# Which engines wait for which output store ahead of the last branch, in a fused attention and maxout kernel on one core

## The chip, the cores and the metric

The kernel runs on one core of a Trainium2 chip. The metric is the device time of one execution in microseconds, and the number compared is the median of several executions.

## The reference

Eight batches of eight heads, sequence length 1024, head size 64; E and F shorten the keys and values from 1024 to 64 rows; a maxout layer follows on the 8192 tokens. The output is 8192 x 512 in float32 (16.8 MB).

```python
k_proj = np.einsum('ks,bhsd->bhkd', E, k)
v_proj = np.einsum('ks,bhsd->bhkd', F, v)
scores = scale * np.matmul(q, k_proj.transpose(0, 1, 3, 2))
attn = softmax(scores)                       # with 1e-9 added to the sum
attn_out = np.matmul(attn, v_proj)           # regrouped to x: 8192 tokens x 512
h1 = x @ w1; h2 = x @ w2                     # 512 -> 1024
out = np.maximum(h1, h2) @ w_out             # 1024 -> 512
```

## The kernel before

**The bulk.** The tokens are worked through in 16 units of 512. For each unit TensorE makes scores, softmax sums, attention outputs, the up products and the down products; the products are built in a scheme with seven block products per pair of matrices (`product`, L747 for the up side, L839 for the down side). ScalarE empties PSUM banks (`keep`, L721) and computes the exponentials, VectorE adds block products (L870, L914, L938) and makes the operand sums. An explicit list of slots (`slots`, `steps`) fixes the order of all instructions on all engines; the change doesn't touch it.

**The last unit.** It is treated apart (`alone`): its output leaves in smaller pieces, so that little is left after the last matmul. `store` (L855) issues one DMA from SBUF to DRAM per piece, on the queue of SyncE (SP) or of ScalarE, and keeps the names of the latest four stores in `ends_of`:

```python
ends_of[:] = [*ends_of[-3:], ins.ins.name]
```

The last five stores are, in order: two of product 3 (128 KB each, on SP and then on ScalarE's queue), and three of product 4 (128 KB on SP, 64 KB on ScalarE's queue, 64 KB on SP). When the program text is complete, `ends_of[0]` is therefore the second store of product 3, on ScalarE's queue; `ends_of[1]` is the 128 KB store of product 4, on SP's queue.

**The guard.** The fast way leaves out the subtraction of the maximum in the softmax. `step_guard` and `step_flag` test the sums of all exponentials and put into `flag` how many rows fell out of a range. At the end every engine loads the flag into a register (L1196 for VectorE, ScalarE and GpSimd, L1180 for SyncE and TensorE, where it stands earlier) and branches on it (L1210): when the flag is zero it jumps over a second, slow version of the whole computation (`tile_shifted`), which has code on all five engines. After the jump each engine has a few semaphore instructions, the program's end barrier (L1363), which SyncE enters only after it has checked the semaphore of every DMA queue and of every engine, and then code that isn't the kernel's.

**The waits ahead of the branch.** Between the register loads and the branch stand three instructions that compute nothing that is used. Each waits for `ends_of[1]`, the third last store, so that its engine comes to the branch only once that store has landed: a one-column matmul on TensorE (L1199), a memset of one element on VectorE (L1200), a copy of one element on ScalarE (L1201). SyncE and GpSimd have no such instruction.

Of the kernel before, what the change touches and what calls it, by code (L numbers as in the profile page):

```python
# [9 lines left out]
FP32 = mybir.dt.float32  # L10
FP16 = mybir.dt.float16
I32 = mybir.dt.int32
# [7 lines left out]
def kernel(  # L20
# [12 lines left out]
    nc = tc.nc  # L33
# [12 lines left out]
    scale = 1.0 / float(D) ** 0.5  # L46

    guard = ctx.enter_context(tc.tile_pool(name="guard", bufs=1))
    flag_ended = guard.tile([1, 4], I32, name="flag")
    flag = flag_ended[:, 0:1]  # L50
    ended = flag_ended.bitcast(FP32)
    outer, ctx = ctx, ExitStack()
    const = ctx.enter_context(tc.tile_pool(name="const", bufs=1))
    kvq = ctx.enter_context(tc.tile_pool(name="kvq", bufs=4))
# [12 lines left out]
    def mm_bank(dtype=FP32, n=None):  # L67
        if n is None:
            n = turn.pop(0)
            turn.append(n)  # L70
        return ps.tile([128, 512 if dtype == FP32 else 1024], dtype, tag=f"mm{n}", name="mm_ps")
# [9 lines left out]
    def big(n, dtype=FP16):  # L81
# [11 lines left out]
            name=nc.get_next_instruction_name(),  # L93
            act_func_set_id=LN_EXP_SET,
            engine=mybir.EngineType.Activation,
            ins=[],
# [33 lines left out]
    for g in range(2):  # L130
        for w_sb, w in ((w2_sb, moe_w2), (w1_sb, moe_w1)):
            nc.gpsimd.dma_start(
                out=w_sb.rearrange("p (g z) f -> p g z f", z=2)[:, g, :, 0:256],
                in_=w.rearrange("(g p z) f -> p g z f", p=128, z=2)[:, g, :, 0:256],
            )
    for w_sb, w, f0, f1 in (
# [3 lines left out]
        for z in range(2):  # L140
            nc.gpsimd.dma_start(
                out=w_sb.rearrange("p (g z) f -> p g z f", z=2)[:, :, z, f0:f1],
                in_=w.rearrange("(g p z) f -> p g z f", p=128, z=2)[:, :, z, f0:f1],
# [3 lines left out]
    ones16 = const.tile([128, 512], FP16)  # L147
# [1034 lines left out]
    ends_of = []  # L1182
# [12 lines left out]
        if reg.engine not in (mybir.EngineType.SP, mybir.EngineType.PE):  # L1195
            nc.reg_load(reg, flag)  # L1196

    for ins in (
        nc.tensor.matmul(out=mm_bank()[0:1, 0:1], lhsT=ones16[:, 0:1], rhs=ones16[:, 0:1], start=True, stop=True),  # L1199
        nc.vector.memset(ended[:, 1:2], 0.0),  # L1200
        nc.scalar.copy(out=ended[:, 2:3], in_=flag),  # L1201
    ):
        for x in ends_of[1:2]:
            tc.add_manual_dep(
                ins.ins, x, mybir.DependencyInfo(mybir.DependencyClass.Sync, mybir.DependencyReason.DATA),
                reason="fetches of instructions wait for the stores",
            )
    ctx.close()

    with tc.If(nc.snap(regs, min_val=0, max_val=256), preferred_fallthrough_block=True, label="shifted"):  # L1210
# [157 lines left out]
```

## Time and profile before

| what | value |
|---|---|
| median of 3 runs | 320.11 us (320.11, 320.11, 320.31) |
| the profiled execution | 320.41 us |
| its span, first to last instruction of the program | 318.6 us |
| around the span | 1.8 us |
| granted TensorE clock | 1.00 |
| TensorE matmul busy | 312.2 us (98%) |
| VectorE, ScalarE busy | 241.3 us (76%), 206.4 us (65%) |
| last matmul of the computation starts, ends | 314.85, 315.13 us |
| the three waiting instructions start | 316.87 to 316.90 us |

The page of the profile gives the busy time of each engine and the chain of work that ended last. Times inside an execution are counted from the start of the span. An engine name with a small q (SPq, DVEq) is that engine's sequencer: branches, semaphore instructions, register loads and the issue of DMAs, none of which counts as busy time.

### The profile page before, as it was taken

The page shows a single profiled execution, that of the slowest core. Times are in us where ns is not written, and L with a number is a line of the kernel's source. Part 1 is how long each engine was busy: PE and PEld are TensorE (multiplying, and loading weights), DVE is VectorE, ACT ScalarE, POOL GpSimd, SP SyncE. Part 2 cuts the span into 40 slices and gives each one's busy share as a digit, 9 for nine tenths or more (in the row PEclk, how much of TensorE's full clock was granted, in tenths as well). Part 3 has the DMA queues.
Part 4 walks back from the last instruction along what each step waited for, and adds up shares of the span by engine and source line. Part 5 has one row for each costly group of instructions (what it writes and reads, how often), then busy time and mean ns, then how long its engine had stood idle before and what let it go on. Part 6 is the DMA issues. An engine that isn't in the chain of part 4 may idle for free.

```text
span 318.6 us, 9311 instructions
## 1 busy us (share of the span) xinstructions
PE 312.2 (98%) x3922; PEld 253.7 (80%) x3922; DVE 241.3 (76%) x442; ACT 206.4 (65%) x374; POOL 40.2 (13%) x63
## 2 busy tenths in 40 slices
PE   8989999999999999999999999999999999999995
PEld 3555588788887888788887888788887888888885
DVE  2365888877969696996969696996969696969873
ACT  2466842777776777477776777477776777765541
POOL 8259002003000300030000400030000000000000
PEclk9999999999999999999999999999999999999999
DMA  7999999999959999899999899989969131313133
GB/s 191 208 198 196 206 206 202 207 167 171 207 109 196 166 208 245 211 178 164 231 222 214 167 205 246 214 145 184 232 145 210 44 102 35 102 35 102 36 115 119
DMA packets 76684, 53.71 MB, mean 169 GB/s; under 512 B 29664, under 2 KB 76128, under 8 KB 76640
## 3 DMA queue, kind: packets, MB, share of 16 engines
q0 software_dynamic: 30688, 28.05, 55.7%
q1 hardware_dynamic: 45664, 24.85, 32.1%
q8 instruction: 31, 0.51, 0.6%
q10 hardware_dynamic: 288, 0.20, 0.2%
q14 instruction: 13, 0.11, 0.1%
HBM read 57.15 MB, written 16.78 MB: 232 GB/s over the span
## 4 chain that ended last, share of the span: by engine, by line
PE 90%; DMA 7%; POOL 1%; DVE 1%; issue 0%; ACT 0%; DVEq 0%; POOLq 0%
PE mm_ps L839 47%; PE mm_ps L747 27%; PE mm_ps L526 4%; DMA q_sb<-in_q_dram 3%; PE att_ps L354 3%; DMA big<-in_moe_w_dram 3%; PE mm_ps L197 3%; PE mm_ps L342 2%; PE mm_ps L635 2%; PE att_ps L239 1%; PE mm_ps L313 1%; DMA out_dram<-o_sb 1%; POOL k_sb L110 0%; DVE xt_sb L445 0%; PE mm_ps L558 0%
## 5 line engine op out<-in xcount | busy, mean ns | idle before, releaser
L721 ACT COPY p_sb<-mm_ps 128x512 f32<-128x512 f32 x179 | 101.8, 592 | 49.0 <-PE mm_ps L747 27.2
L839 PEld LDWEIGHTS <-big 128*128 128x128 f16 x768 | 73.5, 98 | 11.8 <-issue 3.6
L839 PE MATMUL mm_ps<-T_sb,big 128*128 128x256 f16 x576 | 76.9, 273 | 0.0
L762 DVE TENSOR_TENSOR gt_sb<-mm_ps,p_sb 128x512 f16<-128x512 f32 x56 | 38.5, 687 | 43.0 <-PE mm_ps L747 41.6
L747 PE MATMUL mm_ps<-big,big 128*128 128x256 f16 x336 | 50.4, 273 | 0.0
L747 PEld LDWEIGHTS <-big 128*128 128x128 f16 x448 | 43.8, 98 | 5.1
L839 PE MATMUL mm_ps<-wo_sb,gt_sb 128*128 128x256 f16 x256 | 42.6, 273 | 0.0
L839 PEld LDWEIGHTS <-gt_sb 128*128 128x128 f16 x376 | 35.7, 98 | 6.7 <-issue 2.7
L471 ACT ACTIVATE ex_sb<-mm_ps 128x512 f16<-128x512 f32 x50 | 27.2, 596 | 18.0 <-PE mm_ps L342 12.3
L747 PEld LDWEIGHTS <-wd_sb 128*128 128x128 f16 x336 | 32.9, 98 | 3.8
L747 PE MATMUL mm_ps<-xt_sb,wd_sb 128*128 128x256 f16 x224 | 32.8, 273 | 0.0
L501 DVE TENSOR_TENSOR xt_sb<-att_ps,ld_sb 128x1024 f16<-128x1024 f32 x26 | 31.6, 1217 | 0.2
L839 PE MATMUL mm_ps<-m_sb,xt_sb 128*128 128x256 f16 x128 | 24.4, 273 | 0.0
L305 POOL COPY junk<-qt_sb 1x1 f16<-1x1 f16 x6 | 2.0, 340 | 174.1 <-DMA qt_sb<-q_sb 174.1
L870 DVE TENSOR_TENSOR o_sb<-mm_ps,p_sb 128x512 f32<-128x512 f32 x32 | 21.8, 682 | 2.8 <-ACT p_sb L899 2.0
L765 DVE TENSOR_SCALAR gt_sb<-gt_sb 128x512 f16<-128x512 f16 (+1 forms) x60 | 21.1, 351 | 2.1
L707 DVE TENSOR_TENSOR big<-gt_sb 128x1024 f16<-128x1024 f16 x32 | 21.8, 682 | 0.0
L839 PE MATMUL mm_ps<-wo_sb,big 128*128 128x256 f16 x128 | 21.5, 273 | 0.0
L808 ACT ACTIVATE gt_sb<-mm_ps 128x512 f16<-128x512 f32 x28 | 16.8, 601 | 5.7 <-PE mm_ps L747 5.7
L839 PE MATMUL mm_ps<-T_sb,gt_sb 128*128 128x256 f16 x120 | 20.3, 273 | 0.0
L839 PEld LDWEIGHTS <-xt_sb 128*128 128x128 f16 x188 | 18.3, 98 | 2.3 <-issue 0.2
L762 DVE TENSOR_TENSOR gt_sb<-p_sb 128x512 f16<-128x512 f32 x28 | 19.1, 681 | 0.6 <-ACT p_sb L721 0.6
(123 smaller groups left out, 434.2 us busy)
## 6 DMA issues: line engine op xcount, KB each, us to landing
out_dram<-o_sb SPq DMA_DIRECT2D x62, 256.0 KB
k_sb<-in_k_dram POOLq DMA_DIRECT2D x7, 1024.0 KB, 10.0
v_sb<-in_v_dram POOLq DMA_DIRECT2D x7, 1024.0 KB, 16.0
q_sb<-in_q_dram POOLq DMA_DIRECT2D x5, 1024.0 KB, 23.6
q_sb<-in_q_dram POOLq DMA_DIRECT2D x6, 512.0 KB, 15.6
big<-in_moe_w_dram POOLq DMA_DIRECT2D x12, 128.0 KB, 6.4
v_sb<-in_v_dram POOLq DMA_DIRECT2D x4, 256.0 KB, 13.4
wo_sb<-in_moe_w_out_dram POOLq DMA_DIRECT2D x1, 1024.0 KB, 10.1
```

The costliest lines, as they stand in the source:

```text
L197: nc.tensor.matmul(out=kv_ps[r * KP : (r + 1) * KP, h * D : (h + nh) * D], lhsT=eft[i][:, c, :], rhs=t[w][:, h0 + h : h0 + h + nh, c, :], ...
L471: nc.scalar.activation(out=t["ex", g, j][:, e, :], in_=banks[e], func=ACTF.Exp, scale=scale)
L501: nc.vector.tensor_tensor(out=x_out(t, g, j).rearrange("q z o n -> q o z n"), in0=at_ps.rearrange("q o (z n) -> q o z n", z=2), in1=ld[:, ...
L526: nc.tensor.matmul(out=h_ps, lhsT=wd_sb[:, r, fb * 128 : (fb + 1) * 128], rhs=t["xt"][:, r, :, j * W : (j + 1) * W], start=(r == 0), stop= ...
L707: nc.vector.tensor_tensor(out=S(i), in0=S(0) if x is None else x, in1=y(), op=op)
L721: copy(out=x, in_=bank)
L747: nc.tensor.matmul(out=bank[:, m * W : (m + 1) * W], lhsT=w_[:, n_, (2 * d + m) * 128 : (2 * d + m + 1) * 128], rhs=a[:, n_, :], start=(n ...
L762: nc.vector.tensor_tensor(out=c_blk(j, c), in0=two(x), in1=two(y), op=ALU.add)
L765: nc.vector.tensor_scalar_max(ap, ap, 0.0)
L808: nc.scalar.activation(out=out, in_=in_, func=ACTF.Relu)
L839: nc.tensor.matmul(out=bank[i][:, 0:CH] if two_banks else bank[:, i * CH : (i + 1) * CH], lhsT=a(c)[:, i * 128 : (i + 1) * 128], rhs=w_(c) ...
L870: nc.vector.tensor_tensor(out=o_sb, in0=two(x), in1=two(y), op=ALU.add)
```

## The change

VectorE's memset and ScalarE's copy are taken out, with the two views of the flag tile that they wrote to. TensorE's one-column matmul stays where it is, and waits for `ends_of[0]`, the fourth last store (128 KB, on ScalarE's queue), in place of `ends_of[1]` (128 KB, on SP's queue). VectorE and ScalarE go from the load of the flag to the branch with no wait for a store.

```diff
-    flag_ended = guard.tile([1, 4], I32, name="flag")
-    flag = flag_ended[:, 0:1]
-    ended = flag_ended.bitcast(FP32)
+    flag = guard.tile([1, 1], I32, name="flag")
...
-    for ins in (
-        nc.tensor.matmul(out=mm_bank()[0:1, 0:1], lhsT=ones16[:, 0:1], rhs=ones16[:, 0:1], start=True, stop=True),
-        nc.vector.memset(ended[:, 1:2], 0.0),
-        nc.scalar.copy(out=ended[:, 2:3], in_=flag),
-    ):
-        for x in ends_of[1:2]:
-            tc.add_manual_dep(
-                ins.ins, x, mybir.DependencyInfo(mybir.DependencyClass.Sync, mybir.DependencyReason.DATA),
-                reason="fetches of instructions wait for the stores",
-            )
+    ins = nc.tensor.matmul(
+        out=mm_bank()[0:1, 0:1], lhsT=ones16[:, 0:1], rhs=ones16[:, 0:1], start=True, stop=True
+    )
+    tc.add_manual_dep(
+        ins.ins, ends_of[0],
+        mybir.DependencyInfo(mybir.DependencyClass.Sync, mybir.DependencyReason.DATA),
+        reason="a fetch of instructions waits for a store",
+    )
     ctx.close()
```

## The prediction

> **What bounds the kernel now.** I read the page first, to see whether the edit touches what fills the time.
>
> ```profile
> span 318.6 us, 9311 instructions
> ...
> PE 312.2 (98%) x3922; PEld 253.7 (80%) x3922; DVE 241.3 (76%) x442; ACT 206.4 (65%) x374; POOL 40.2 (13%) x63
> ...
> PE 90%; DMA 7%; POOL 1%; DVE 1%; issue 0%; ACT 0%; DVEq 0%; POOLq 0%
> ```
>
> TensorE bounds the kernel, and the edit takes no matmul from it: up to the last matmul of the computation (ends 315.13) nothing differs. What can move is the last 3.5 us of the span (315.13 to 318.63) and the 1.78 us around it (320.41 - 318.63). So the second view is the chain of waits for the end:
>
> ```profile
> 314.55 0.65 DVE o_sb L938 x3
> 315.20 1.72 DMA out_dram<-o_sb
> 316.93 0.17 ACT flag L1201
> ```
>
> The end hangs on stores in flight. The list of waits from 314 us on says which instructions they hold, and what SyncE's own queue waits for:
>
> ```profile
> ACT flag L1201 <- DMA out_dram<-o_sb: 3.0, 1, 3.0
> PEld L1199 <- DMA out_dram<-o_sb: 1.9, 1, 1.9
> ...
> DVE flag L1200 <- DMA out_dram<-o_sb: 1.4, 1, 1.4
> ...
> SPq L1363 <- DVEq L1210: 0.5, 1, 0.5
> ```
>
> The last line is the one that matters: SyncE, checking everything before the end barrier, stands 0.5 us for VectorE's first instruction after the branch, not for a DMA. The busy times by stretch show whether data still moves by then:
>
> ```profile
> 315.90:316.30 0.40, 0.00 (x0) 0.00 (x0) 0.00 (x0) 0.00 (x0) 0.00 (x0) 1.00 0.99 320
> 316.30:316.90 0.60, 0.03 (x1) 0.03 (x1) 0.03 (x1) 0.00 (x0) 0.00 (x0) 1.00 0.78 212
> 316.90:317.20 0.30, 0.14 (x1) 0.05 (x1) 0.03 (x1) 0.19 (x1) 0.00 (x0) 1.00 0.00 0
> 317.20:317.90 0.70, 0.00 (x0) 0.00 (x0) 0.00 (x0) 0.00 (x0) 0.00 (x0) 1.00 0.00 0
> ```
>
> The last two columns are DMA share and GB/s: the last store's packets are through by 316.9. The semaphore updates in the trace give when each store had landed: the fourth last at 316.28, the third last at 316.83, the last two at 317.01 and 317.20. The sequencers' rows at the branch:
>
> ```profile
> L1210 DVEq COMPARE_BRANCH x1: 72/72/72, 316.9 to 316.9; - x1
> L1210 PEldq COMPARE_BRANCH x1: 383/383/383, 317.0 to 317.0; - x1
> ...
> L1210 ACTq EVENT_SEMAPHORE  x1: 17/17/17, 317.5 to 317.5; - x1
> L1210 DVEq EVENT_SEMAPHORE  x1: 21/21/21, 317.5 to 317.5; - x1
> ```
>
> VectorE branches at 316.94 (until 317.01) and runs its next instruction only at 317.54; ScalarE 316.99 and 317.46; TensorE 316.97 (383 ns) and 317.41. Last, the DMA view from 316.9 us to the end, for code fetches:
>
> ```profile
> DMA  0000000000000000000000000906000004000000
> ...
> q8 instruction: 1, 0.02, 4.0%
> q14 instruction: 2, 0.02, 2.8%
> ```
>
> A slice is 43 ns, and a packet counts where it starts: 16 KB of code starts at 318.00, 1.03 us after TensorE's branch begins; two of 8 KB start at 318.05 and 318.33. Queue 8 is TensorE's: its 31 packets bring 0.51 MB in the whole run, 65 bytes for each of TensorE's 7844 instructions; the other engines' code comes in the 8 KB packets. Here a 16 KB packet takes 4.0% x 16 x 1.7 us = 1.09 us, an 8 KB one 2.8% x 16 x 1.7 / 2 = 0.38 us.
>
> **The change, part by part.**
>
> *VectorE's memset out.* 59 ns by itself; what counts is its wait. The flag load runs 315.18 to 315.75, so the branch moves from 316.94 to about 315.9, and with the same 0.53 us behind it VectorE is through at about 316.5. SyncE asks for this at 317.08: the 0.51 us stand (317.08 to 317.59) goes. What is late next is the last store: SyncE's checks follow each other by 62 ns, it would ask for that store at 317.14, and it lands at 317.20. Then come the same steps as now: SyncE's last drain at 317.42 instead of 317.82, so the span is **0.40 us** shorter. The barrier behind it (318.63 - 317.82 = 0.81 us) stays.
>
> *ScalarE's wait and copy out.* 17 and 190 ns. The flag load ends at 316.27, the branch comes near 316.4, the first instruction after it 0.42 to 0.5 us later, at 316.9. SyncE asks for it last, at 317.29. Nothing, while 0.4 us of cover stands; left in place, the wait would give a release at 317.49, so it would have to go with VectorE's.
>
> *TensorE waits for the fourth last store.* Landed at 316.28 instead of 316.83: 0.55 us earlier. With 40 ns to react as now, branch at 316.42 to 316.80, next instruction at 316.86. SyncE's check on TensorE stands beside the last store's, so the span gains nothing more. Nothing of the computation is queued behind the matmul on TensorE. But the code fetch moves with the branch, from 318.00 to 317.45, through at 318.54 instead of 319.09.
>
> *Behind the span.* No instruction of the kernel is there, only semaphore updates: a signal passes from engine to engine twice. Its hops in the second round are 34, 38, 45 ns; in the first 34, **207**, 44. The 207 ns hop ends at 319.10, 9 ns after TensorE's fetch. If the fetch holds it, it comes at 318.55, so 0.55 us earlier, and the shorter span allows 318.86 - 0.40 + 0.07 = 318.53. If something else does, it moves with the span, by 0.40 us. The fetch fits to 9 ns, but one hop is little evidence: I take **0.50 us**, nearer to the fetch's row.
>
> [...]
>
> *The flag tile, 4 bytes instead of 16.* No row prices it; one element is read at a time. Nothing.
>
> Sum: 320.41 - 0.50 = 319.91 in the profiled execution. That one lies 0.30 us above the median, so 320.11 - 0.50 = **319.6 us**, 0.16% less. The bounds: 0.40 and 0.57 us (the hop at 318.53), so 319.5 to 319.75 for this case alone. A measurement of this kernel tells about 0.2%, 0.64 us, from no change: the forecast is a gain that hardly shows.
>
> **The rivals.**
>
> *The gain passes the bound: 319.4.* After the first round each engine clears a block of semaphores; the block that starts last does so at 319.61, 0.22 us after the round's end, where the others need at most 0.07. If this too waits for code (an 8 KB fetch starts late, at 318.84, and ends at 319.28), up to 0.15 us more can go: 0.57 + 0.15 = 0.72. For it: the fetches overlap each other here, and TensorE's takes 1.09 us where the mean of the 31 is 0.6% x 16 x 318.6 / 31 = 0.99; apart they should be shorter. Against it: nothing ties that block to a fetch.
>
> *Hidden anyway: 320.1.* SyncE needs the last store at 317.20; were that 0.39 us later, it would stand until 317.59 as now. VectorE's fetch, 1.0 to 1.4 us after a branch at 315.9, starts at 316.9 to 317.3, just when the last packets (316.85) are through. Some 0.1 us earlier, its 0.38 us fall on one DMA engine's share of that store, and eat the span's gain. Here belongs also that the edit doesn't do what it says: were ScalarE's queue drained late, TensorE would leave no sooner than now. Against both: its store landed 0.55 us before the other.
>
> *Slower: 320.8.* TensorE's own fetch falls before the last store. The 16 KB packet takes 1.09 us; put ahead of the last packets on one DMA engine it moves the landing from 317.20 to 318.29, and SyncE's release from 317.59 to 318.29, 0.70 us later than now. It decides from a fetch start before 316.85, that is within 0.43 us of the branch at 316.42. For it: the DMA engines are at a share of 0.78 to 0.99 until then, and the new wait lets TensorE go at 316.3, when 0.6 us of store packets are still to move. Against it: the fetch came 1.03 us after the branch. [...]
>
> **How the numbers follow.** Forecast 0.42; hidden anyway 0.13; both are within 0.2%, together 0.55. Gain past the bound 0.28: its terms are few and I know one execution. Slower 0.17. The range runs from the larger gain, with 0.1 us for the spread of the medians, to no gain with the 0.3 us that the profiled execution lay above: 319.3 to 320.4. It leaves out the slower case.
>
> **What would show it.** Right: in the changed profile SyncE's wait for VectorE's branch is gone from its list and the longest is for the last store; TensorE's matmul at L1199 starts at 316.3; the 16 KB fetch starts at about 317.45 in an empty DMA row; the span is 318.2. Wrong: a code fetch among the last store's packets; a landing later than 317.3; or a time around the span that differs from 1.7 us by over 0.15 us.

## The result and the profile after

The medians are 319.96 us after (319.64 to 320.28, 22 runs) and 320.40 us before (320.11 to 321.23, 22 runs). The ratio is 0.9983 with a 95% interval of 0.9977 to 0.9990: 0.54 us faster, 0.32 to 0.74 us (the two medians by themselves differ by 0.44 us). A ratio of 1 lies outside the interval; the gain itself lies under the 0.2% (0.64 us) below which the prediction took a gain to be hard to see. The profiled execution took 319.90 us, with a span of

```profile
span 318.1 us, 9308 instructions
```

The list of what SyncE's queue waits for, from 314 us on (columns: us in total, times, longest us), is where the change shows:

```profile
SPq L853 <- DVE o_sb L936: 0.9, 1, 0.9
SPq L1359 <- SPq L1359: 0.4, 1, 0.4
SPq L1359 <- PEq L1359: 0.3, 1, 0.3
SPq L1206 <- SPq L1206: 0.2, 1, 0.2
```

The line of the kernel before in which SyncE stood 0.5 us for VectorE's first instruction after the branch is gone. The lines left are the issue of the last stores (L853), the end barrier (L1359) and SyncE's own steps behind its branch (L1206), as before. A wait for the last store has no line here, because it is short: by the trace, SyncE's check for it stands 134 ns behind the one before, where 62 ns is the usual step, and 17 ns behind the landing. The sequencers' rows at the branch (L1206, count, durations in ns, first and last start):

```profile
L1206 DVEq COMPARE_BRANCH x1: 72/72/72, 315.8 to 315.8; - x1
...
L1206 ACTq COMPARE_BRANCH x1: 54/54/54, 316.3 to 316.3; - x1
L1206 PEldq COMPARE_BRANCH x1: 388/388/388, 316.3 to 316.3; - x1
L1206 DVEq EVENT_SEMAPHORE  x1: 21/21/21, 316.4 to 316.4; - x1
L1206 PEldq EVENT_SEMAPHORE  x1: 51/51/51, 316.8 to 316.8; - x1
L1206 ACTq EVENT_SEMAPHORE  x1: 17/17/17, 316.8 to 316.8; - x1
```

All three engines have run their first instruction behind the branch by 316.83; the last store landed at 317.10. The busy times by stretch (DMA share and GB/s last) and the DMA view from 316.9 to 318.6 us (slices of 43 ns) show what became of the code fetches:

```profile
316.30:316.90 0.60, 0.10 (x1) 0.01 (x1) 0.00 (x0) 0.00 (x0) 0.00 (x0) 1.00 0.63 163
316.90:317.20 0.30, 0.00 (x0) 0.00 (x0) 0.00 (x0) 0.00 (x0) 0.00 (x0) 1.00 0.14 27
```

```profile
DMA  0090000000060000000000090000000007000000
...
q14 instruction: 3, 0.02, 6.2%
q8 instruction: 1, 0.02, 3.3%
```

Three fetches of 8 KB start at 317.03, 317.41 and 318.34, and TensorE's 16 KB at 317.88. The first follows the last store packet (316.75) by 0.28 us.

Where the time went is told by one interval: from the landing of the last store to the end of the span. It was 318.63 - 317.20 = **1.43 us** before and is 318.12 - 317.10 = **1.02 us** after, 0.41 us less. The other 0.10 us between the two spans is that the last store landed earlier in the second execution; over the nine profiled executions in which that store took 1.71 or 1.72 us, it landed anywhere from 316.96 to 317.36. The time around the span is 1.78 us in both.

### The profile page after: what moved, and what is told of

Its sections match the earlier page's. It is cut to its first block, busy times and chain, and to the rows that moved or that the text cites. A ratio compares the mean times of both kernels' runs of the same rounds, so it can differ in the third digit from the quotient of the medians.

```text
span 318.1 us, 9308 instructions
## 1 busy us (share of the span) xinstructions
PE 312.3 (98%) x3922; PEld 253.6 (80%) x3922; DVE 241.1 (76%) x441; ACT 206.2 (65%) x373; POOL 40.8 (13%) x63
## 4 chain that ended last, share of the span: by engine, by line
PE 92%; DMA 5%; POOL 1%; ACT 1%; issue 0%; DVE 0%; POOLq 0%
PE mm_ps L837 47%; PE mm_ps L745 27%; PE mm_ps L524 4%; DMA v_sb<-in_v_dram 4%; PE att_ps L352 3%; PE mm_ps L195 3%; PE mm_ps L340 2%; PE mm_ps L633 2%; PE att_ps L237 1%; DMA out_dram<-o_sb 1%; PE mm_ps L311 1%; POOL k_sb L108 0%; POOL q_sb L108 0%; ACT ld_sb L388 0%; ACT ex_sb L380 0%
```

## The experiments

Theory A: the end of the span is set by SyncE's list of checks, so by whatever on it is satisfied last: VectorE's, TensorE's or ScalarE's first instruction behind the branch, or the last store. Rival B: TensorE's earlier branch and code fetch carry the gain. Rival C: code fetches among the stores hold them up, so that too early a branch costs. For each kernel the table gives, from its profiled execution, the time from the last store's issue to its landing, from the landing to the end of the span, and the ratio to the kernel before, from all its runs. The edits are shown shortened, and the first one in words.

| kernel | issue to landing | landing to end | ratio [95%] |
|---|---|---|---|
| before | 1.72 us | 1.43 us | 1 |
| changed | 1.71 | 1.02 | 0.9983 [0.9977, 0.9990] |
| changed, again | 1.72 | 1.02 | 0.9993 [0.9975, 1.0011] |
| only TensorE moved | 1.72 | 1.42 | 1.0012 [1.0003, 1.0021] |
| VectorE's and ScalarE's out | 1.72 | 1.28 | 1.0001 [0.9992, 1.0010] |
| VectorE's out | 1.71 | 1.26 | 1.0001 [0.9992, 1.0010] |
| changed, ScalarE waits | 1.72 | 1.22 | 0.9985 [0.9960, 1.0009] |
| all wait for the last store | 1.72 | 1.80 | 1.0007 [0.9981, 1.0032] |
| changed, TensorE for the fifth last | 1.72 | 1.02 | 0.9978 [0.9954, 1.0002] |
| changed, VectorE loads early | 2.57 | 1.02 | 1.0011 [0.9986, 1.0035] |
| changed, no wait at all | 3.63 | 1.02 | 1.0059 [1.0045, 1.0072] |
| before, TensorE free | 3.71 | 1.02 | 1.0049 [1.0032, 1.0066] |

Wide intervals come from single outlying runs (up to 323.84 us); what the ratios leave unclear is read from the second and third columns, which come from one execution of each kernel and leave out all that happens before the last store's issue.

**Only TensorE's wait moved.**

```diff
-        nc.tensor.matmul(...)  waits for ends_of[1]
+        nc.tensor.matmul(...)  waits for ends_of[0]
         nc.vector.memset(...)  waits for ends_of[1]
         nc.scalar.copy(...)    waits for ends_of[1]
```

> Only TensorE's matmul moves to the fourth last store; VectorE and ScalarE still wait for the third last. From the last store's landing to the end of the span it was 1.43 us in the kernel before and 1.02 in the changed one. Theory A, SyncE's list of checks: the check on VectorE still ends last, so 1.43 us again and no gain (within 0.1 us of the kernel before). Rival B, TensorE's earlier branch carries the gain: 0.2 to 0.45 us faster, with the 16 KB fetch and the end of the execution earlier.

SyncE's list still has its 0.5 us:

```profile
SPq L1362 <- DVEq L1209: 0.5, 1, 0.5
```

The interval is 1.42 us; TensorE branched at 316.52 and its fetch started at 317.55, and nothing came of it. B falls. The median is 0.24 us above that of the kernel before, by an interval that leaves out zero; the one profiled execution (320.50 us) shows no place for that, and it stays open.

**VectorE's and ScalarE's instructions out, TensorE's as before.**

```diff
-        nc.vector.memset(ended[:, 1:2], 0.0),
-        nc.scalar.copy(out=ended[:, 2:3], in_=flag),
```

> VectorE's memset and ScalarE's copy are out, TensorE still waits for the third last store. Theory A: SyncE passes VectorE at once and then stands for TensorE, whose first instruction after the branch raised its semaphore 0.09 us before VectorE's did in the kernel before; the span is about 0.12 us shorter (1.31 us behind the last landing), a third of the change's gain. Rival B: no gain at all, since TensorE branches as before. Rival D, VectorE's and ScalarE's waits alone are worth it all: the full 0.4 us.

```profile
SPq L1360 <- PEq L1207: 0.4, 1, 0.4
```

As A has it, SyncE now stands for TensorE, 0.4 us in place of 0.5; the interval is 1.28 us, a gain of 0.15 us that the ratio can't show. Two of the three waits alone are worth a third of the gain.

**VectorE's instruction out.** As above, with ScalarE's copy left in.

> Only VectorE's memset is out; TensorE and ScalarE wait for the third last store as in the kernel before. Theory A: the same 0.12 us as with ScalarE's copy out too (1.31 us behind the last landing), since TensorE's check comes ahead of ScalarE's and holds both. Rival D: the full 0.4 us.

1.26 us, and the same line for TensorE in SyncE's list. Again A; VectorE's wait is not worth it all.

**The changed kernel with ScalarE's wait.** TensorE on the fourth last store, VectorE free, ScalarE's copy kept on the third last.

> As the changed kernel, but ScalarE's copy stays and waits for the third last store. Theory A, SyncE's list: ScalarE's first instruction after the branch comes at about 317.47 as in the kernel before, SyncE asks for it last and gets it there; about 1.23 us from the last landing to the end of the span, between the kernel before (1.43) and the changed one (1.02), so half of the gain. Rival: ScalarE's wait is covered and costs nothing, 1.02 us.

```profile
SPq L1361 <- ACTq L1208: 0.2, 1, 0.2
```

1.22 us: half of the gain, with ScalarE now the last on the list. So TensorE's wait holds the end when VectorE is free, and ScalarE's when the other two are out of the way; that VectorE's does follows from the first run, where its check ends last and costs 0.2 us more than ScalarE's alone. Only with all three out of the way is it the store.

**All three wait for the last store.**

```diff
-        for x in ends_of[1:2]:
+        for x in ends_of[3:4]:
```

> As the kernel before, but all three instructions wait for the last store (landed 317.20) in place of the third last (316.83). Theory A: VectorE's branch and SyncE's release move by the same 0.37 us, 1.80 us from the last landing to the end of the span, 0.37 us slower than the kernel before. Rival E, later branches are cheaper than they look because fetches meet no store: less than 0.15 us slower.

```profile
SPq L1362 <- DVEq L1209: 0.9, 1, 0.9
```

1.80 us, to the hundredth what A said; the medians differ by 0.5 us (320.94 and 320.43), though the interval of the ratio includes 1. E falls by SyncE's list, not by the times.

**No wait at all.** The matmul stays, without its dependency.

```diff
-    tc.add_manual_dep(ins.ins, ends_of[0], ...)
```

> As the changed kernel, but TensorE's matmul waits for no store either, so TensorE branches at about 315.3 us, before the last four stores have moved. Theory A: nothing more to gain, 1.02 us behind the last landing, the changed kernel's time. Rival C, the code fetch falls among the stores: a 16 KB packet of 0.9 to 1.1 us stands ahead of store packets on one DMA engine, the last store lands 0.4 to 1.1 us later after its issue (1.72 us in the kernel before) and the time is 0.4 to 1.1 us longer than the changed kernel's.

```profile
SPq L1354 <- DMA out_dram<-o_sb: 2.0, 1, 2.0
```

The median is 322.13 us, 1.7 us above the kernel before. TensorE branched at 315.34. The other packets of the last stores were through at 316.86, but nine of them, 4 KB, a sixteenth of the last store's 144 packets, moved only from 317.97 to 318.45, and the store landed at 319.13, 3.63 us after its issue. SyncE stands 2.0 us for it. C holds as far as it goes, but the landing is 1.91 us late where 0.4 to 1.1 us were expected, and all three engines fetch code here, so this run doesn't tell whose fetch it is.

**The kernel before with TensorE alone set free.** VectorE and ScalarE keep their waits.

> As the kernel before, but TensorE's matmul waits for no store; VectorE and ScalarE still wait for the third last, so that TensorE's 16 KB fetch is the only one among the stores. With no wait and all three fetches early the last store landed 3.63 us after its issue in place of 1.72, its late packets moving from 317.97 on, when all three fetches were through. Theory F1, TensorE's fetch alone does it: the landing is 0.9 to 1.3 us late (one packet of 0.9 to 1.1 us and the order behind it), 1.02 us from it to the end. Theory F2, the 8 KB fetches of the other two hold the store as much: with them kept back the landing is late by less than 0.6 us, and the time is within 0.3 us of the kernel before.

The GB/s row of its DMA view from 315.3 to 319.3 us (slices of 0.1 us):

```profile
GB/s 328 164 82 307 369 328 292 272 282 256 261 139 5 0 0 164 0 0 0 0 0 0 0 5 5 174 10 5 5 0 0 0 0 0 0 0 0 0 0 0
...
q8 instruction: 1, 0.02, 1.4%
```

The store packets end at 316.54; then comes the 16 KB fetch (316.83 to 317.71, slice 16), and only then, at 5 to 10 GB/s, the nine packets left over. The two 8 KB fetches (slice 26) come at 317.81, too late to have held these packets back. So TensorE's early branch and its fetch do it alone, as F1 says, but the landing is 1.98 us late and not 0.9 to 1.3: the nine packets don't move while the fetch is under way nor in the 0.29 us before its packet, and they land 0.66 us after the last of them where 0.35 us is usual. The parts add up: 0.29 us ahead of the fetch's packet, 0.86 until the first of the nine starts (317.70), 0.53 for the nine, 0.31 of later landing. Why nothing moves in the first of these parts, and why the landing takes longer, the trace doesn't show. The fetch's one packet took 0.88 us, less than half of the delay measured.

**TensorE waits for the fifth last store.**

```diff
-                ends_of[:] = [*ends_of[-3:], ins.ins.name]
+                ends_of[:] = [*ends_of[-4:], ins.ins.name]
```

> As the changed kernel, but TensorE waits for the fifth last store (landed at 315.9 us), so it branches at about 316.0, 0.35 us sooner. By theory A nothing is gained (1.02 us behind the last landing, the changed kernel's time), as long as the code fetch stays out of the last store. With 1.03 us from a free branch to its fetch (kernel before, and TensorE's wait moved alone), the fetch would start at 317.05, after the last packets at 316.8, and the time is the changed kernel's. Rival C2, what counts is when the fetch is asked for, not when its packet starts: asked for while store packets are still queued, it goes ahead of one DMA engine's share of the last store, which then lands about 2 us later as without any wait, and the time is 1.5 to 2.2 us longer.

```profile
GB/s 338 277 92 184 317 348 318 297 292 277 272 251 67 0 0 164 82 0 0 82 0 0 0 0 0 0 0 0 0 0 82 0 0 0 0 0 0 0 0 0
```

The same slices as above: the stores are through at 316.61, the fetch starts at 316.88 (slice 16), 1.04 us after the branch at 315.85, and nothing is left over. 1.02 us, the changed kernel's. C2 falls for this branch: 0.77 us ahead of the end of the store packets it is still harmless. The two branches that did harm came 1.52 us (no wait) and 1.47 us (TensorE free) ahead of the end of the other store packets.

**VectorE loads the flag earlier.**

```diff
-        at = {SP: ("U", last - 1, 1, 4), PE: ("P", last, 5, 0)}.get(reg.engine)
+        at = {SP: ("U", last - 1, 1, 4), PE: ("P", last, 5, 0), DVE: ("P", last, 5, 0)}.get(reg.engine)
```

> As the changed kernel, but VectorE loads the flag earlier, in the third last product, as TensorE does, so that VectorE branches at about 315.2 to 315.3 us in place of 315.8; its 8 KB fetch then is asked for 0.5 us sooner, among the last stores. Theory A without collision: the changed kernel's time, 1.02 us behind the last landing. Rival C, an 8 KB fetch (0.4 to 0.7 us) goes ahead of one DMA engine's share of the last store: the last landing 0.4 to 1.5 us later, and the time as much longer.

```profile
SPq L853 <- DVE o_sb L936: 1.3, 1, 1.3
SPq L1360 <- DMA out_dram<-o_sb: 0.9, 2, 0.8
```

VectorE branched at 314.98 and its 8 KB fetch started at 316.50, among the store packets. The last store landed 2.57 us after its issue, 0.85 us late. The load itself made VectorE's last additions, and with them the issue of the last three stores, later: the first two by 0.32 us, the last by 0.28 (SyncE waits 1.3 us for an addition in the first line, 0.9 in the other kernels). With the 0.41 us of the changed kernel that makes 0.28 + 0.85 - 0.41 = 0.72 us; the medians differ by 0.78 us. So an 8 KB fetch among the stores goes with a late landing too: nine packets of the store before the last, a sixteenth of it, move only from 316.87 on, when the fetch ends, and nine of the last store behind them, from 317.18 to 317.50. But TensorE's 16 KB fetch starts at 317.17 and runs beside those last packets, which then land 0.56 us behind the last of them and not 0.35. How the 0.85 us divide between the two fetches isn't shown.

**The changed kernel again.**

> The changed kernel once more, on the chip and beside the runs of this call. By SyncE's list 1.02 us from the last landing to the end of the span, 0.4 us less than the kernel before, ratio 0.9987; if half of the measured gain was the chip's or the day's, 0.2 us or less.

The medians are 320.00 and 320.31 us; the ratio is unclear (one run of 322.72 us). The medians by themselves, 0.31 us apart, lie between the two expectations. The interval of 1.02 us is that of the first execution to 1 ns, so the 0.41 us at the end of the span belong to the code.

## Why the prediction was right, step by step

*The step from VectorE's check to the last store* was to take 0.40 us from the span. Measured: 0.41. Branch and next instruction came at 315.81 and 316.41 (315.9 and 316.5 were worked out), SyncE's last drain 0.22 us after the last landing, as the 62 ns steps gave. Of the signs that the prediction named, VectorE's line is gone from SyncE's list, TensorE's matmul started at 316.23 (316.3) and the span is 318.1 us (318.2). The wait for the last store is too short to stand in the list, and the time around the span stayed at 1.78 us and didn't come down to 1.7.

*The share of the three edits* was told wrongly. The prediction gave the whole to VectorE and wrote that TensorE's wait adds nothing to the span. It is worth nothing alone (1.42), but VectorE's alone is worth 0.16 us, because TensorE would be next on the list at 317.5. The prediction named this cover for ScalarE, with its release at 317.49, and the run with ScalarE's wait bears it out (1.22); for TensorE it forgot it. The smaller flag tile isn't where the rest lies: the kernel before with TensorE alone set free has the old tile, and 1.02 us once the store is last.

*The code fetch* was to move with the branch to 317.45. It came at 317.88, 1.55 us after the branch, in a row with three other fetches and not in an empty one. An 8 KB fetch (317.41, 0.47 us) ended at that moment, but that isn't shown to be the cause: in the second execution of the same kernel TensorE's fetch started at 317.62, 1.05 us after its branch, with an 8 KB fetch still under way (317.24 to 317.74). The prediction's 1.03 us holds to 0.02 us in eight of the twelve executions; the others are 1.53 (all three wait for the last store), 1.55 here, and 1.64 and 1.77 us in the two collisions.

*The late hop behind the span* was the one term that failed: 0.10 us were booked for it. The hop is 208 ns in the changed kernel too, ending at 318.59, before the fetch is through (318.79); it is 207 or 208 ns in every kernel here, whatever the fetch does. So it is no wait for that fetch; the 9 ns were a coincidence. The sum should have been 0.40 us; the forecast of 0.50 lies inside the measured 0.32 to 0.74, and so does 0.41, so that the times alone couldn't have told the two apart.

*The forecast of 319.6 us* stands on the median of three runs, 320.11 us. The 22 runs beside the changed kernel give 320.40 us for the kernel before, so the profiled execution of 320.41 us didn't lie 0.30 us high: the base was 0.29 us low. With 320.40 us for the base and 0.40 us for the gain the sum is 320.00 us, next to the measured 319.96. That value lies outside the narrow bounds of 319.5 to 319.75 us and inside the stated range only because of its upper part, which was meant for a gain that stays hidden: for the time itself that is luck, for the gain it isn't.

*The first instructions behind the branch* didn't wait for a code fetch in the executions named here. In the kernel before, TensorE ran on at 317.41 and its fetch started at 318.00; without any wait it ran on at 315.79, 1.2 us before its fetch started. The kernel marks this branch as likely taken for TensorE; what the mark does isn't shown, since every run has it. VectorE has no such mark, and in the changed kernel it ran on at 316.41, while no code fetch stands in the trace between 303.0 and 317.03. What the 0.53 us behind its branch are, the same in eleven of the twelve executions, stays open.

*The rivals.* More than the bound: nothing came out of the time around the span, 1.77 to 1.86 us in all. Hidden anyway: the first 8 KB fetch, taken as VectorE's, missed the last packets by 0.28 us. Slower: too early a branch of TensorE does make the last store land late, but that was priced at less than half: 0.70 us worked out, 1.6 and 1.7 us measured. The 0.70 us stand on an estimate, that the fetch delays the landing by the 1.09 us of its own packet; no run shows a delay of that size: with TensorE free the packet took 0.88 us and the landing came 1.98 us late. The sign given for it, a fetch that starts before the last packets, isn't what the runs show: in the two runs in which TensorE branched too early, its fetch's packet itself started late, 0.12 and 0.29 us behind the other store packets. What tells the cases apart is the branch. With 1.03 us from branch to fetch the bound would be a branch 1.03 us ahead of the end of the store packets, and the runs put it between 0.77 us (harmless) and 1.47 us (held). The changed kernel's TensorE branches 0.41 us ahead.

## What to carry to other kernels

When an end barrier checks a list, write down when each entry is ready: taking out the latest gains only down to the next, so edits that are worthless or small alone (0.01 and 0.15 us here) can be worth more together (0.41). A wait that computes nothing may still be holding back a code fetch (TensorE's started at 318.00, with its wait moved at 317.55, with none at 316.83): the question is then not whether to wait, but which early event is enough; here waiting for the fifth last store was enough, and waiting for none cost 1.7 us. And compare the ends of two executions from a common event (the last landing), since that interval repeats to 0.01 us where whole times spread by 0.6 us.

## What was not expected of the hardware

With TensorE's branch early, a 16 KB code fetch of 0.88 us went with a delay of 1.98 us for a 64 KB store, through 4 KB of it in nine packets; with VectorE's early, an 8 KB fetch, and TensorE's behind it, went with 0.85 us. The hop of 207 or 208 ns in the signal behind the program is the same in all twelve executions.
